# Transposes of first-stage tiles and expert blocks: 32x32 blocks on VectorE, placed by loads from DRAM

## The chip, the core and the metric

The kernel runs on one core of a Trainium2 chip. The metric is the device time of one execution in microseconds (us). The engines are TensorE (PE, its weight loads are PEld), VectorE (DVE), ScalarE (ACT), GpSimd (POOL), and SyncE (SP), which here issues most of the transfers; a queue issue stands as SPq.

## The reference

Three layers follow each other on 8 sequences of 3072 tokens with 256 channels, all in float32:

```
Y = rfft(x, axis=1) * (filt_r + 1j*filt_i);  y = irfft(Y)          # along the sequence
xn = y / sqrt(mean(y*y) + 1e-6) * rms_g                             # 24576 tokens
z  = (silu(xn @ w_gate) * (xn @ w_val)) @ w_out                     # 256 -> 1536 -> 256
e  = argmax(z @ w_route); p = softmax(z @ w_route)[e]               # 8 experts, one per token
out = p * (max(z @ w1[e], 0) @ w2[e])                               # 256 -> 1024 -> 256
```

## The kernel before

Accuracy of float32 is had by splitting each operand into a high and a low part (`split`: ACT writes the high part, DVE or POOL the difference) and by three matmuls for each product (`mm3`, lines 93 to 95).

**First stage.** The tokens go in 48 tiles of 512. For each tile the f loop has 12 turns, one for each 128 columns of the hidden layer: `gv(f)` makes 12 matmuls of 512 columns into two PSUM buffers r, `act(f)` turns them into s, ph and pl (lines 504, 505, 89, 90), and `z(f-1)` takes 12 matmuls of 264 columns with ph and pl of the turn before. PE's program therefore reads gv(f), z(f-1), gv(f+1), z(f). Beside it run the transform of the next sequence (`Job`, with forward steps, inverse steps and first steps, each with its own loads and stores on SP), and the preparation of the next tile (`Front`), in steps that a table puts on turns of the loop: `FRONT_V` holds those ahead of gv, `FRONT_P` those of PE behind z. Step 3 (turn 6) brings the tile to SBUF as x with tokens on the partitions and starts the RMS. Step 4 (turn 8) scales x by 1/rms (line 463) and has SP copy it to xc (line 468), which is the form in which PE takes it in one pass. Steps 5 and 7 (turns 9 and 10, line 478) transpose four 128x128 pieces each on PE into a PSUM buffer, and steps 6 and 8 (turns 10 and 11, lines 483 and 484) make xth on ACT and xtl on DVE from it, with rms_g. These are the moving operands of the next tile's gv. Tile 0 is prepared ahead of the loop and transposes x itself (line 480).

At the end of a tile its rows (256 values, 8 expert scores, the token's number) are scattered by POOL to zs in DRAM, sorted by expert.

**Experts.** 256 rows of one expert are a block. `run` takes the blocks in turn; each has four steps s with 12 matmuls of h and 12 of y (256 columns each), so PE's program reads h(s), y(s-1). The load of the block after next is issued in step 0 (`load`, line 731, the tile brow), behind that block's weight transfers (lines 719 and 720), which move data only where the expert changes. Step 1 transposes the next block by four 128x128 pieces on PE behind y (`tr`, line 768), step 2 splits the result into zth and ztl (`trs`), and makes the gate (`gate`, lines 753 to 761). The relu output is hh on ACT and hl on DVE (lines 785 and 786). 100 blocks run; the first four are taken from the leading expert while the last tiles are still at work.

All instructions of an engine run in the order of the program (`manual_schedule`): nothing overtakes a waiting one on the same engine. On SP this holds for the issue of transfers as well.

Of the kernel before, what the change touches and what calls it, by code (L numbers as in the profile page):

```python
# [10 lines left out]
F32 = mybir.dt.float32  # L11
# [8 lines left out]
D = 256  # L20
SEQ = 3072
FF = 1536
NE = 8
# [11 lines left out]
def fft_moe_moe_kernel(  # L35
# [33 lines left out]
    def rot():  # L69
        return psr.tile([128, 512], F32, tag="r", name="r")  # L70
# [347 lines left out]
    class Front:  # L418
# [4 lines left out]
        def step(self, k):  # L423
            if k == 0:
                z = zb[self.b]
                self.zr = []
                for a in range(2):
                    r = bp.tile([128, 2, D], F32, tag="xr", name="zr")
                    n0 = 4 * self.tau + 2 * a
                    nc.sync.dma_start(r, z[n0:n0 + 2].rearrange("n r d -> r n d"))  # L430
                    self.zr.append(r)
            elif k == 1:
                self.zh, self.zl = [], []
                for a in range(2 if self.t else 0):
                    h = bp.tile([128, 2, D], FR, tag="zh", name="zh")
                    l = bp.tile([128, 2, D], FR, tag="zl", name="zl")
                    split(h, l, self.zr[a])
                    self.zh.append(h)
                    self.zl.append(l)
            elif k == 2:  # L440
                self.q = []
                for a in range(2):
                    q = rot()
                    if self.t:
                        mm3(q, dft_h[:, 128:256], dft_l[:, 128:256], self.zh[a], self.zl[a], True, True)
                    else:
                        nc.tensor.matmul(q, lhsT=dft_raw[:, 128:256], rhs=self.zr[a], start=True, stop=True)
                    self.q.append(q)
            elif k == 3:
                self.x = bp.tile([128, 4, D], F32, tag="x", name="x", bufs=1)  # L450
                for a in range(2):
                    nc.vector.tensor_copy(self.x[:, 2 * a:2 * a + 2], self.q[a].rearrange("p (a d) -> p a d", a=2))  # L452
                ss = bp.tile([128, 4], F32, tag="ss", name="ss")
                for a in range(4):
                    junk = bp.tile([128, D], F32, tag="junk", name="junk", bufs=1)
                    nc.scalar.activation(junk, self.x[:, a], AF.Square, accum_out=ss[:, a:a + 1])
                self.ms = bp.tile([128, 4], F32, tag="ms", name="ms")
                nc.gpsimd.tensor_scalar(self.ms, ss, 1.0 / D, 1e-6, op0=ALU.mult, op1=ALU.add)
                self.ri = bp.tile([128, 4], F32, tag="ri", name="ri")
                nc.gpsimd.tensor_tensor(self.ri, self.ms, mhalf, op=ALU.pow)  # L460
            elif k == 4:
                for a in range(4):
                    nc.vector.tensor_scalar(self.x[:, a], self.x[:, a], self.ri[:, a:a + 1], None, op0=ALU.mult)
                if self.t:
                    self.xc = []
                    for a in range(2):
                        r = bp.tile([128, 2, D], F32, tag="xr", name="xc")
                        nc.sync.dma_start(r, self.x[:, 2 * a:2 * a + 2])
                        self.xc.append(r)
                self.h = bp.tile([128, 2, 512], FR, tag="xth", name="xth")  # L470
                self.l = bp.tile([128, 2, 512], FR, tag="xtl", name="xtl")
            elif k in (5, 7):
                c = (k - 5) // 2
                self.qt = rot()
                for a in range(4):
                    o, d = self.qt[:, a * 128:(a + 1) * 128], slice(c * 128, (c + 1) * 128)
                    if self.t:
                        nc.tensor.transpose(o.bitcast(FR), self.xc[a // 2][:, a % 2, d].bitcast(FR), idfr)
                    else:
                        nc.tensor.transpose(o, self.x[:, a, d], ident)  # L480
            elif k in (6, 8):
                c = (k - 6) // 2
                nc.scalar.activation(self.h[:, c], self.qt, AF.Copy, scale=rmsg[:, c:c + 1])
                nc.vector.scalar_tensor_tensor(self.l[:, c], self.qt, rmsg[:, c:c + 1], self.h[:, c].bitcast(F32), op0=ALU.mult, op1=ALU.subtract)

    class Mid:
        def __init__(self, fr):
# [212 lines left out]
    class Blk:  # L700
        def __init__(self, n):
            self.n = n
            self.side = (n + 1 - EARLY) % 2 if n >= EARLY else 0
            self.row = None

        @property
        def w(self):
# [14 lines left out]
        def load(self):  # L722
            if self.row is not None:
                return
            if self.n < EARLY:
                rb = nc.sync.value_load(esti[0:1, 0:1], min_val=0, max_val=(NE - 1) * CAP) + self.n * BLK
            else:
                i = self.n - EARLY
                rb = nc.sync.value_load(bti[i:i + 1, 0:1], min_val=0, max_val=NE * CAP)
            self.row = cpa.tile([128, 2, RW], F32, tag="row", name="brow", bufs=3)  # L730
            nc.sync.dma_start(self.row, zs[bass.ds(rb, BLK), :].rearrange("(p t) w -> p t w", t=2))

        def fresh(self):
            return self.n == 0 or self.n >= EARLY
# [12 lines left out]
            e.tensor_tensor(l, r, h.bitcast(F32), op=ALU.subtract)  # L747

        def gate(self):
            lg = self.row[:, :, D:WX]  # L750
# [10 lines left out]
            nc.vector.tensor_copy(self.id, self.row[:, :, WX])  # L761

        def tr(self):
            self.qt = rot()
            for c in range(2):
                for a in range(2):
                    j = 2 * c + a
                    nc.tensor.transpose(self.qt[:, j * 128:(j + 1) * 128].bitcast(FR), self.row[:, a, c * 128:(c + 1) * 128].bitcast(FR), idfr)

        def trs(self):  # L770
            self.zh = cpa.tile([128, 2, BLK], FR, tag="zth", name="zth")
            self.zl = cpa.tile([128, 2, BLK], FR, tag="ztl", name="ztl")
            split(self.zh, self.zl, self.qt.rearrange("p (c t) -> p c t", c=2))

        def h(self, s):
            self.q = rot()
# [32 lines left out]
                tc.add_to_no_dep_group("outs", i.ins)  # L809

    cpa = None
    blks = [Blk(n) for n in range(NBLK)]

    def early(t, f):
# [69 lines left out]
    prev.evac()  # L884

    def settle(k):
        if k == 0:
            prev.route(0)
        elif k == 1:
# [4 lines left out]
        elif k < 6:  # L894
            table(k - 2)
        elif k == 6:
            ab.close()
            cpb = ctx.enter_context(tc.tile_pool(name="cpb", bufs=1, reuse_waits="tile"))
            par[1] = wset(cpb, 1)
            sent[0] = cpb.tile([128, 2, RW], F32, name="sent")  # L900
            nc.gpsimd.memset(sent[0][:, :, 0:WX], 0.0)
            nc.gpsimd.tensor_scalar(sent[0][:, :, WX], cstt[:, 12:14], float(NTOK), None, op0=ALU.add)
# [100 lines left out]
def _constants(nb):  # L1003
# [5 lines left out]
    c[:, 4:8] = 24 * p[:, None] + np.arange(4)  # L1009
    c[:, 8] = p  # L1010
    c[:, 10] = p - 2
    c[:, 12:14] = 2 * p[:, None] + np.arange(2)
# [53 lines left out]
```

## Time and profile before

| | |
|---|---|
| median of 3 runs | 4168.78 us (4168.57 to 4171.68) |
| span of the profiled execution | 4165.9 us |
| PE busy | 4061.6 us (97%), 26476 matmuls |
| PEld busy | 3670.7 us (88%) |
| DVE busy | 2667.1 us (64%) |
| ACT busy | 2048.1 us (49%) |
| POOL busy | 1120.7 us (27%) |
| mean granted clock of TensorE | 0.989 |

The span is that of one execution on the chip, from its first to its last instruction. The busy time of an engine is the union of its instructions; a matmul's record reaches to its modelled end, so the next one starts before it is over, and the price of a matmul is better read from starts. In a timeline row the first number is the start, the second the duration (or the stretch of several merged instructions, with their count at the end), and in brackets stands how long the engine was idle before and what released it. The first stage's loop lasts to about 2975 us, the blocks from there to the end.

### The profile page before, as it was taken

The numbers are of one execution on the slowest core, as the hardware profiler recorded it, in microseconds if no ns is written. First come the engines' busy times: TensorE is split into PE (matmuls) and PEld (weight loads), VectorE is DVE, ScalarE is ACT, GpSimd is POOL, SyncE is SP. The second block draws the span as 40 slices with busy tenths as digits, with TensorE's granted clock in tenths as the row PEclk, the third lists the DMA queues.
The fourth block names the chain that finished last, engine by engine and source line by source line (L and its number), as shares of the span: only waits on it lengthen the run. The fifth ranks groups of instructions, "written<-read, shape, count | busy, mean of one in ns | idle before, by whom it ended". The sixth has DMA issues, their size and how long they took to land. (4 is left out here: it accounts for less than half of the span.)

```text
span 4165.9 us, 71195 instructions
## 1 busy us (share of the span) xinstructions
PE 4061.6 (97%) x26476; PEld 3670.7 (88%) x26476; DVE 2667.1 (64%) x5108; ACT 2048.1 (49%) x4027; POOL 1120.7 (27%) x1030
## 2 busy tenths in 40 slices
PE   4899999999999999999999999999999999999998
PEld 2688888888888888888888888888999999999998
DVE  7557657646755754774665576454477777777775
ACT  2344444444444444444444444343366666666665
POOL 5313112212212310321231122111144444444443
PEclk7899999999999999999999999999999999999999
DMA  8234233223323423322332332101222212221221
GB/s 234 90 103 116 76 91 104 82 88 86 93 80 89 106 63 96 95 79 91 100 91 68 93 99 67 47 32 37 70 68 85 87 57 77 86 87 61 70 84 39
DMA packets 196240, 350.52 MB, mean 84 GB/s; under 512 B 21930, under 2 KB 88750, under 8 KB 195888
## 3 DMA queue, kind: packets, MB, share of 16 engines
q1 hardware_dynamic: 174288, 287.33, 24.1%
q0 software_dynamic: 18816, 51.25, 3.5%
q10 hardware_dynamic: 2784, 7.34, 0.6%
q8 instruction: 210, 3.44, 0.4%
q14 instruction: 142, 1.16, 0.1%
HBM read 384.96 MB, written 105.04 MB: 118 GB/s over the span
## 5 line engine op out<-in xcount | busy, mean ns | idle before, releaser
L89 ACT ACTIVATE ph<-s 128x512 fp32r<-128x512 f32 x576 | 364.0, 632 | 1003.2 <-DVE s L505 1003.2
L505 DVE TENSOR_TENSOR s<-s,r 128x512 f32<-128x512 f32 x576 | 394.4, 685 | 524.9 <-PE r L95 497.9
L90 DVE TENSOR_TENSOR pl<-s,ph 128x512 fp32r<-128x512 f32 x576 | 439.4, 763 | 402.0 <-ACT ph L89 402.0
L95 PE MATMUL z<-wo_h,pl 128*128 128x264 f32 x2304 | 659.1, 286 | 5.2 <-DVE pl L90 5.0
L93 PE MATMUL z<-wo_h,ph 128*128 128x264 f32 x2304 | 656.3, 285 | 3.8 <-ACT ph L89 3.4
L94 PE MATMUL z<-wo_l,ph 128*128 128x264 f32 x2304 | 656.9, 285 | 0.0
L560 POOL DMA_INDIRECT zs<-row,di x192 | 206.0, 1073 | 1340.4 <-DVE di L558 635.4
L504 ACT ACTIVATE s<-r 128x512 f32<-128x512 f32 x576 | 342.6, 595 | 346.0 <-PE r L95 344.4
L93 PE MATMUL r<-xth,wg_h 128*128 128x512 f32 x1152 | 467.1, 405 | 0.4 <-DVE s L505 0.4
L93 PEld LDWEIGHTS z<-wo_h,ph 128*128 128x128 f32 x2304 | 434.7, 189 | 35.7 <-ACT ph L89 10.0
L93 PE MATMUL r<-xth,wv_h 128*128 128x512 f32 x1152 | 456.3, 396 | 2.5 <-DVE x L452 2.2
L93 PE MATMUL r<-zth,w1h 128*128 128x256 f32 x1600 | 455.6, 285 | 0.4 <-DVE hl L786 0.4
L94 PE MATMUL r<-xtl,wg_h 128*128 128x512 f32 x1152 | 455.9, 396 | 0.0
L95 PE MATMUL r<-xth,wg_l 128*128 128x512 f32 x1152 | 455.7, 396 | 0.0
L94 PE MATMUL r<-xtl,wv_h 128*128 128x512 f32 x1152 | 455.5, 395 | 0.0
L94 PEld LDWEIGHTS z<-wo_l,ph 128*128 128x128 f32 x2304 | 433.6, 188 | 24.2
L95 PE MATMUL r<-xth,wv_l 128*128 128x512 f32 x1152 | 454.6, 395 | 0.0
L94 PE MATMUL y<-w2l,hh 128*128 128x256 f32 x1600 | 450.9, 282 | 0.0
L95 PE MATMUL y<-w2h,hl 128*128 128x256 f32 x1600 | 449.9, 281 | 0.2 <-DVE hl L786 0.2
L95 PE MATMUL r<-zth,w1l 128*128 128x256 f32 x1600 | 449.5, 281 | 0.0
L93 PE MATMUL y<-w2h,hh 128*128 128x256 f32 x1600 | 448.9, 281 | 0.0
L94 PE MATMUL r<-ztl,w1h 128*128 128x256 f32 x1600 | 448.6, 280 | 0.0
(188 smaller groups left out, 9176.8 us busy)
## 6 DMA issues: line engine op xcount, KB each, us to landing
w1r<-in_w_dram SPq DMA_DIRECT2D x97, 1024.0 KB
w2r<-in_w_dram SPq DMA_DIRECT2D x97, 1024.0 KB
tab<-in_tab_dram SPq DMA_DIRECT2D x128, 528.0 KB
brow<-zs SPq DMA_DIRECT2D x100, 265.0 KB
fin<-in_x_dram SPq DMA_DIRECT2D x96, 256.0 KB
s<-fo SPq DMA_DIRECT2D x96, 256.0 KB
fin<-s SPq DMA_DIRECT2D x128, 192.0 KB
z<-fo SPq DMA_DIRECT2D x128, 192.0 KB
```

Source lines behind the costliest of these rows:

```text
L89: nc.scalar.activation(hi, src, AF.Copy)
L90: e.tensor_tensor(lo, src, hi.bitcast(F32), op=ALU.subtract)
L93: nc.tensor.matmul(o, lhsT=lh, rhs=rh, start=first, stop=False)
L94: nc.tensor.matmul(o, lhsT=lh, rhs=rl, start=False, stop=False)
L95: nc.tensor.matmul(o, lhsT=ll, rhs=rh, start=False, stop=last)
L504: nc.scalar.activation(s, self.q[0], AF.Silu)
L505: nc.vector.tensor_tensor(s, s, self.q[1], op=ALU.mult)
L560: i = nc.gpsimd.indirect_dma_start(out=zs[:, :], out_offset=bass.IndirectOffsetOnAxis(ap=di[:, t:t + 1], axis=0), in_=self.row[:, t, :], i ...
```

## The change

In a first-stage tile (but not in tile 0) step 4 now scales x and transposes it on VectorE, in 32x32 blocks, one instruction for each half of the channels, into xt. Each half goes to a buffer xs in DRAM, and four loads, one for each 32 channels of a half, bring the blocks back to where a full transpose has them, in xd. Steps 5 and 7 are gone for these tiles, and steps 6 and 8 read xd in SBUF where they read PSUM. The order of the tokens within a tile is another now, and the numbers that are written with them follow it (`_constants`).

A block from the fifth on (`turned`) is loaded in nine pieces: ext with the scores and the number, and eight of 32 partitions with 128 bytes each in zp, which place the 32x32 blocks; `tr` is then one VectorE instruction from zp to zd, and `trs` reads zd. The tiles zp and ext have three buffers in a pool of their own.

```
 (Front.step, k == 4)
-                    self.xc = []
-                    for a in range(2):
-                        r = bp.tile([128, 2, D], F32, tag="xr", name="xc")
-                        nc.sync.dma_start(r, self.x[:, 2 * a:2 * a + 2])
-                        self.xc.append(r)
+                    xs = dram.tile([128, 2, 4, 128], F32, tag="xs", name="xs", bufs=2)
+                    xd = bp.tile([128, 2, 4, 128], F32, tag="x", name="xd", bufs=1)
+                    for c in range(2):
+                        r = bp.tile([128, 4, 4, 32], F32, tag="xr", name="xt")
+                        nc.vector.transpose(r.rearrange("p j n b -> p n j b"), self.x[:, :, c * 128:(c + 1) * 128])
+                        nc.sync.dma_start(xs[:, c], r.rearrange("p j n b -> p j (n b)"))
+                    for j in range(4):
+                        nc.sync.dma_start(xd[32 * j:32 * j + 32], xs[:, :, j].rearrange("(i a) c r -> a c i r", i=4))
+                    self.xd = xd
...
-            elif k in (5, 7):
+            elif k in (5, 7) and self.t == 0:
...
+                v = self.xd[:, c].rearrange("p i r -> p (i r)") if self.t else self.qt
-                nc.scalar.activation(self.h[:, c], self.qt, AF.Copy, scale=rmsg[:, c:c + 1])
+                nc.scalar.activation(self.h[:, c], v, AF.Copy, scale=rmsg[:, c:c + 1])
...
-    FRONT_P = {5: 2, 9: 5, 10: 7}
+    FRONT_P = {5: 2}
 (Blk.load)
-            self.row = cpa.tile([128, 2, RW], F32, tag="row", name="brow", bufs=3)
-            nc.sync.dma_start(self.row, zs[bass.ds(rb, BLK), :].rearrange("(p t) w -> p t w", t=2))
+            rows = zs[bass.ds(rb, BLK), :].rearrange("(t p) w -> p t w", t=2)
...
+            self.row = turn.tile([128, 2, RW - D], F32, tag="ext", name="ext")
+            self.zp = turn.tile([128, 2, 8, 32], F32, tag="zp", name="zp")
+            nc.sync.dma_start(self.row, rows[:, :, D:RW])
+            self.ext = self.row
+            cols = zs[bass.ds(rb, BLK), :].rearrange("(q b) w -> b q w", b=32)
+            for j in range(4):
+                for c in range(2):
+                    d = c * 128 + j * 32
+                    nc.sync.dma_start(self.zp[32 * j:32 * j + 32, c], cols[:, :, d:d + 32])
 (Blk.tr)
+            if self.turned:
+                self.zd = cpa.tile([128, 2, BLK], F32, tag="zd", name="zd", bufs=1)
+                nc.vector.transpose(self.zd, self.zp)
+                return
```

On SP, the first turned tile: xs is the buffer in DRAM, xd the tile that comes back, fin the background transform's input.

```order
 L152 DMA wraw<-in_w_val_dram 128x1024 x2
-L468 DMA xc<-x 128x512 x2
+L470 DMA xs<-xt 128x512 x2
+L472 DMA xd<-xs 32x8x128 x4
 L260 DMA fin<-in_x_dram 128x512 x5
```

Two stores and four loads stand where the two copies stood, ahead of the same loads of the background.

On DVE, a later tile of the first stage, around step 4, first before, then after:

```order
L463 TENSOR_SCALAR x<-x,ri 128x256 x4
L505 TENSOR_TENSOR s<-s,r 128x512
L90 TENSOR_TENSOR pl<-s,ph 128x512
L505 TENSOR_TENSOR s<-s,r 128x512
L90 TENSOR_TENSOR pl<-s,ph 128x512
L484 SCALAR_TENSOR_TENSOR xtl<-r,rmsg,xth 128x512
```

```order
L463 TENSOR_SCALAR x<-x,ri 128x256 x4
L469 STREAM_TRANSPOSE xt<-x 128x4x4x32 x2
L507 TENSOR_TENSOR s<-s,r 128x512
L90 TENSOR_TENSOR pl<-s,ph 128x512
L507 TENSOR_TENSOR s<-s,r 128x512
L90 TENSOR_TENSOR pl<-s,ph 128x512
L486 SCALAR_TENSOR_TENSOR xtl<-xd,rmsg,xth 128x512
```

The two transposes stand between the scaling and the s of the same turn, two turns ahead of xtl.

On DVE, an expert block, steps 0 to 2, first before, then after:

```order
L803 TENSOR_SCALAR yo<-y_34994,gw 128x256
L747 TENSOR_TENSOR w1l_27585<-w1r_27588,w1h_27584 128x512 x2
L786 SCALAR_TENSOR_TENSOR hl<-r,hh 128x512
L90 TENSOR_TENSOR ztl<-r,zth 128x512
L747 TENSOR_TENSOR w2l_27587<-w2r_27589,w2h_27586 128x512
```

```order
L823 TENSOR_SCALAR yo<-y_35029,gw 128x256
L763 TENSOR_TENSOR w1l_27501<-w1r_27504,w1h_27500 128x512 x2
L806 SCALAR_TENSOR_TENSOR hl<-r,hh 128x512
L782 STREAM_TRANSPOSE zd<-zp 128x512
L90 TENSOR_TENSOR ztl<-zd,zth 128x512
L763 TENSOR_TENSOR w2l_27503<-w2r_27505,w2h_27502 128x512
```

The transpose of the next block stands between the hl of step 1 and the ztl of step 2.

## Rows read from the trace of the kernel before

**Rows 1.** Busy time by stretch: us, engines (xinstructions), granted clock, DMA share, GB/s.

```profile
400.00:2900.00 2500.00, 2485.57 (x14409) 2171.16 (x14408) 1524.42 (x2838) 1107.76 (x2179) 502.85 (x503) 1.00 0.28 82
3100.00:4000.00 900.00, 900.00 (x7665) 900.00 (x7664) 658.35 (x1380) 590.78 (x1150) 367.09 (x307) 1.00 0.25 77
```

**Rows 2.** Groups of instructions: busy us, mean ns of one, idle before.

```profile
L768 PE MATMUL r<-idfr,brow 128*128 128x128 f32 x400 | 45.8, 237 | 0.0
```

**Rows 3.** Timeline of an expert block, PE, and DVE's hl of step 2.

```profile
3407.58 0.29 PE L95 MATMUL y<-w2h,hl 128*128 128x256 f32 x1
...
3408.31 0.28 PE L95 MATMUL r<-zth,w1l 128*128 128x256 f32 x1
...
3410.37 0.69 DVE L786 SCALAR_TENSOR_TENSOR hl<-r,hh 128x512 fp32r<-128x512 f32 x1 [0.24 <-ACT hh L785]
...
3412.26 0.29 PE L95 MATMUL r<-zth,w1l 128*128 128x256 f32 x1
...
3412.63 0.28 PE L95 MATMUL y<-w2h,hl 128*128 128x256 f32 x1
```

**Rows 4.** Timeline of PE in the first stage, turns with and without transposes.

```profile
1526.33 0.29 PE L95 MATMUL z<-wo_h,pl 128*128 128x264 f32 x1
...
1527.28 0.39 PE L95 MATMUL r<-xth,wg_l 128*128 128x512 f32 x1
...
1535.58 0.28 PE L95 MATMUL z<-wo_h,pl 128*128 128x264 f32 x1
...
1536.16 0.39 PE L95 MATMUL r<-xth,wg_l 128*128 128x512 f32 x1
```

**Rows 5.** Timeline of a tile without background steps: DVE, ACT and PE.

```profile
2641.69 1.14 DVE L463 TENSOR_SCALAR x<-x,ri 128x256 f32<-128x256 f32 x4
...
2649.90 0.69 ACT L483 ACTIVATE xth<-r,rmsg 128x512 fp32r<-128x512 f32 x1 [0.35 <-PE r L478]
2651.43 0.60 ACT L504 ACTIVATE s<-r 128x512 f32<-128x512 f32 x1 [0.85 <-PE r L95]
2653.56 0.63 ACT L89 ACTIVATE ph<-s 128x512 fp32r<-128x512 f32 x1 [1.52 <-DVE s L505]
...
2657.18 0.29 PE L93 MATMUL z<-wo_h,ph 128*128 128x264 f32 x1
```

**Rows 6.** Groups of instructions on DVE: busy us, mean ns, idle before.

```profile
L347 DVE SCALAR_TENSOR_TENSOR sw<-sw,cstt,tab 96x512 f32<-96x512 f32 x112 | 124.9, 1115 | 0.0
L345 DVE STREAM_SHUFFLE sw<-r 96x512 f32<-96x512 f32 x112 | 83.0, 741 | 0.0
```

**Rows 7.** Timeline of a tile with a forward step behind the scaling: DVE and PE.

```profile
1337.39 2.94 DVE L463 TENSOR_SCALAR x<-x,ri 128x256 f32<-128x256 f32 x4
...
1344.23 0.69 DVE L90 TENSOR_TENSOR pl<-s,ph 128x512 fp32r<-128x512 f32 x1 [0.70 <-ACT ph L89]
...
1344.98 0.39 PE L95 MATMUL z<-wo_h,pl 128*128 128x264 f32 x1 [0.20 <-DVE pl L90]
```

**Rows 8.** Waits: who for whom, us in total, times, longest.

```profile
DVE gid L761 <- DMA out_dram<-yo,gid: 16.4, 16, 2.0
```

**Rows 9.** Timeline of SP and PE at the first tile: a store, its reload, first use.

```profile
139.48 0.30 SPq L375 DMA_DIRECT2D z<-fo  x1
...
141.95 0.89 SPq L430 DMA_DIRECT2D zr<-z  x2
...
145.65 3.75 PE L447 MATMUL r<-zr,dft_raw 128*128 128x512 f32 x4 [6.88 <-DMA zr<-z]
```

**Rows 10.** The page's first line, and its queues: packets, MB, share of 16 engines.

```profile
span 4165.9 us, 71195 instructions
...
q1 hardware_dynamic: 174288, 287.33, 24.1%
```

**Rows 11.** DMA of the stretch from 3.0 to 4.2 us: packets, then its one queue.

```profile
DMA packets 517, 0.06 MB, mean 49 GB/s; under 512 B 492, under 2 KB 493, under 8 KB 517
...
q1 hardware_dynamic: 517, 0.06, 47.1%
```

More of the change, by code (lines that the diff above doesn't have):

```diff
@@ L470, in step @@
+                    for j in range(4):
+                        nc.sync.dma_start(xd[32 * j:32 * j + 32], xs[:, :, j].rearrange("(i a) c r -> a c i r", i=4))
+                    self.xd = xd
                 self.h = bp.tile([128, 2, 512], FR, tag="xth", name="xth")
                 self.l = bp.tile([128, 2, 512], FR, tag="xtl", name="xtl")
-            elif k in (5, 7):
+            elif k in (5, 7) and self.t == 0:
                 c = (k - 5) // 2
                 self.qt = rot()
+                qv = self.qt.rearrange("p (i n b) -> p n i b", i=4, n=4)
@@ L475, in step @@
                 for a in range(4):
[L476 to L480, printed above, removed]
+                    nc.tensor.transpose(qv[:, a], self.x[:, a, c * 128:(c + 1) * 128], ident)
             elif k in (6, 8):
                 c = (k - 6) // 2
-                nc.scalar.activation(self.h[:, c], self.qt, AF.Copy, scale=rmsg[:, c:c + 1])
@@ L484, in step @@
-                nc.vector.scalar_tensor_tensor(self.l[:, c], self.qt, rmsg[:, c:c + 1], self.h[:, c].bitcast(F32), op0=ALU.mult, op1=ALU.subtract)
+                v = self.xd[:, c].rearrange("p i r -> p (i r)") if self.t else self.qt
+                nc.scalar.activation(self.h[:, c], v, AF.Copy, scale=rmsg[:, c:c + 1])
+                nc.vector.scalar_tensor_tensor(self.l[:, c], v, rmsg[:, c:c + 1], self.h[:, c].bitcast(F32), op0=ALU.mult, op1=ALU.subtract)
     class Mid:
@@ L704, in __init__ @@
             self.row = None
+            self.turned = n > 3
         @property
@@ L729, in load @@
                 rb = nc.sync.value_load(bti[i:i + 1, 0:1], min_val=0, max_val=NE * CAP)
-            self.row = cpa.tile([128, 2, RW], F32, tag="row", name="brow", bufs=3)
-            nc.sync.dma_start(self.row, zs[bass.ds(rb, BLK), :].rearrange("(p t) w -> p t w", t=2))
+            rows = zs[bass.ds(rb, BLK), :].rearrange("(t p) w -> p t w", t=2)
+            if not self.turned:
+                self.row = cpa.tile([128, 2, RW], F32, tag="row", name="brow", bufs=2)
+                nc.sync.dma_start(self.row, rows)
+                self.ext = self.row[:, :, D:RW]
+                return
[8 more added lines that the diff above has]
+                    nc.sync.dma_start(self.zp[32 * j:32 * j + 32, c], cols[:, :, d:d + 32])
         def fresh(self):
@@ L749, in gate @@
         def gate(self):
-            lg = self.row[:, :, D:WX]
+            lg = self.ext[:, :, 0:NE]
             m = cpa.tile([128, 2], F32, tag="gm", name="gm")
@@ L760, in gate @@
             self.id = cpa.tile([128, 2], I32, tag="gid", name="gid")
-            nc.vector.tensor_copy(self.id, self.row[:, :, WX])
+            nc.vector.tensor_copy(self.id, self.ext[:, :, NE])
         def tr(self):
+            if self.turned:
+                self.zd = cpa.tile([128, 2, BLK], F32, tag="zd", name="zd", bufs=1)
+                nc.vector.transpose(self.zd, self.zp)
+                return
             self.qt = rot()
@@ L772, in trs @@
             self.zl = cpa.tile([128, 2, BLK], FR, tag="ztl", name="ztl")
-            split(self.zh, self.zl, self.qt.rearrange("p (c t) -> p c t", c=2))
+            split(self.zh, self.zl, self.zd if self.turned else self.qt.rearrange("p (c t) -> p c t", c=2))
         def h(self, s):
@@ L811, in fft_moe_moe_kernel @@
     cpa = None
+    turn = None
     blks = [Blk(n) for n in range(NBLK)]
@@ L886, in settle @@
     def settle(k):
+        nonlocal turn
         if k == 0:
@@ L899, in settle @@
             par[1] = wset(cpb, 1)
+            turn = ctx.enter_context(tc.tile_pool(name="turn", bufs=3, reuse_waits="tile"))
             sent[0] = cpb.tile([128, 2, RW], F32, name="sent")
@@ L1008, in _constants @@
     c[:, 0] = np.where(p % 2 == 0, -1.0, 1.0)
-    c[:, 4:8] = 24 * p[:, None] + np.arange(4)
+    c[:, 4:8] = 24 * (32 * np.arange(4) + p[:, None] % 32) + p[:, None] // 32
     c[:, 8] = p
```

## The prediction

> **What bounds the kernel now.** I read the busy time by stretch first. In the 900 us of the expert stage TensorE is busy for all 900, in 2500 us of the first stage for 2485.6, so 14.4 us are idle there, and the granted clock is 1.00 in both, which is the upper of its two levels, 2.4 GHz [rows 1]. VectorE is busy 61% and 73% of the same stretches. So both stages last as long as TensorE's instruction list, as long as nothing that feeds it comes later than now. A matmul that leaves that list is worth the time by which it holds up the next ones; it is worth nothing only where another wait takes its place. Then I read what the transposes hold up, in TensorE's timeline. Last I read what stands around the places where the new work goes: VectorE and ScalarE in a first-stage tile and VectorE in an expert block.
>
> **What is removed.** From the first stage 376 transposes go, 4 at each of two places in 47 tiles: 94 groups. The blocks have 400 [rows 2], in 100 groups; the first four blocks keep theirs, so 96 groups go. The union of the busy times (45.8 us for the 400) is not the price, because matmuls overlap. I take starts instead, from the last matmul ahead of a group to the third one behind it.
> Expert block: 3407.58 to 3408.31 is 0.73 us with four transposes between; three steps without any, 3412.26 to 3412.63, take 0.37 [rows 3]. Price 0.36 us, times 96 = 34.6 us.
> First stage: 1526.33 to 1527.28 is 0.95; the same step without transposes, 1535.58 to 1536.16, is 0.58 [rows 4]. Price 0.37, times 94 = 34.8 us.
> Together 69.4 us, all of it on the path, since TensorE has no gap at these places. The two copies of x on SP go too, and one PSUM buffer per group comes free; I count neither.
>
> **What is added on VectorE.** Two block transposes of 128x512 behind the four scalings in each tile, and one in each of the 96 blocks. The trace has no such operation. Nearest is the lane shuffle of 96x512, 741 ns; above it lies the costliest 96x512 operation, 1115 ns on average; below it the scaling, four of 128x256 in 1.14 us, thus 0.57 us for 512 columns [rows 5, 6]. I take 0.74, since the shuffle is the one that moves data between lanes, with 0.57 and 1.12 as ends.
> The Trainium skill, "VectorE: DVE Perf Modes", section "The three transpose paths", gives 311 ns for a 128x128 transpose in bf16 on VectorE and, in its rules for kernel authors, advises TensorE for a 128x128 one if the result may lie in PSUM. Four times 311 ns is an estimate of 1.24 us for 512 columns; the sum with it would be 12 to 15 us less gain. No run here shows it yet.
>
> In a first-stage tile the 1.48 us push VectorE's next products back. Mostly there is idle time: in the tile at 2641 VectorE waits before its next s. In four tiles there is none (near 630, 691, 1345 and 2476 us): a forward step of the background transform stands right behind the scaling, and from 1337.39 to the end of pl at 1344.92 VectorE and the s, ph, pl chain have no slack; TensorE waits 0.20 us for this pl already [rows 7]. There all 1.48 us reach TensorE: 4 x 1.48 = 5.9 us lost (4.6 to 9.0 at the ends). Five more tiles with the same step have about 1.4 us to spare; from 0.72 us a transpose they begin to pay, up to 5 us at 1.12. That is in the range only.
>
> In an expert block the transpose stands behind one hl and ahead of ztl. The next hl ends at 3411.06 and is read first at 3412.63, 1.57 us later [rows 3]. If all 0.74 us went into that and TensorE comes 0.36 earlier, 0.47 us remain; at 1.12 still 0.09. Cost 0.
> One more place in the blocks: 16 times VectorE waits 1.0 us for a scatter before gid [rows 8], and that wait doesn't move with TensorE. There the gain may be given back: between 0 and 16 x 0.36 = 5.8 us. I take the middle, 2.9.
>
> **What is added on SP.** In a tile, six transfers stand where two stood: two stores to DRAM, which wait for VectorE, and four loads, which wait for the stores; the background's stores and loads queue behind them. In the tile at 2641 the scaling ends at 2642.83, the second transpose at 2644.3. From the issue of a store to the issue of the load that waits for it: 139.48 to 141.95, 2.47 us. From the issue of a load to the first matmul on it: 141.95 to 145.65, 3.70 us, with other loads in the queue; I take 2.47 as the lower end. Two issues take 0.89 us, so the fourth load goes out 1.35 us behind the first [rows 9]. Data there at 2644.3 + 2.47 + 1.35 + 2.47 to 3.70 = 2650.6 to 2651.8. ScalarE turns to xth at 2649.90, so it will stand 0.7 to 1.9 us. What covers that: 0.84 us up to its next s at 2651.43, and ph, which ends at 2654.19 and is read at 2657.18, 2.99 us later; TensorE comes 2 x 0.37 earlier [rows 5]. Cover 3.1 us, thus 1.2 left at worst. Cost 0; each us past the cover costs 47 us over the tiles.
> Behind these six, the background's loads slip by some 5 us; they are issued four steps ahead of use (a step is at least a 4 us turn of the f loop), and its stores have two buffers. Cost 0.
> In a block, nine transfers stand where one stood, 8 x 0.45 = 3.6 us more of SP in a block of some 11.4. The load is for the block after next, more than a block ahead of its transpose. Behind it stand the next block's weight transfers, which move data only where the expert changes. Cost 0; if that cover goes, a few us in all.
>
> **The sum.** 34.6 + 34.8 - 5.9 - 2.9 = 60.6 us. The profiled execution has a span of 4165.9 us [rows 10], the median of the runs is 4168.8, 2.9 us more, which the change doesn't touch. 4168.8 - 60.6 = 4108.2 us.
>
> **The rivals.**
> (a) Round trip too slow, the one that can end slower. If the two legs through DRAM take longer than above because stores, filter tables and spectrum traffic share the queue, data come after the cover's end. It decides at 3.1 us past 2649.90; at 4.4 us past, 1.3 x 47 = 61 us, the gain is gone; at 5.1 us past it costs 94, thus 4202 us. For it: 1.2 us is not much, and both legs are from one place. Against: the load's leg was measured beside other traffic, and where a background step lies between the scaling and xth, which it doesn't in this tile, the turns of the loop are longer.
> (b) Small pieces bound the blocks. A block's load becomes 2048 pieces of 128 bytes and 256 of 36. At the mean price of a packet of this queue, 24.1% of 16 x 4165.9 us over 174288 = 92 ns [rows 10], 2304 pieces take 13.3 us of the 16 engines. A block has 100 of the 7665 matmuls of 900 us, so it lasts 11.74 us now [rows 1] and 11.38 by the forecast: 1.9 x 96 = 182 us more, thus 4290. Against: in the 1.2 us from 3.0 on, 517 packets, 492 of them under 512 bytes, took 47.1% of the engines, 17.5 ns each [rows 11]; at that price a block takes 2.5 us.
> The Trainium skill, "DMA: Bandwidth & Descriptors", section "Specifications", names 512 bytes as the least transfer for line rate and a read-modify-write below it. By that rule the time would be (b)'s; the row on small packets speaks against it.
> (c) A dear transpose on VectorE, 1.24 us: the four tiles pay 9.9, five others 5.4, three more 2, gid 5.8: 69.4 - 23 = 46, thus 4122 us.
> (d) The change does nothing: TensorE's list gets shorter but another wait fills it. Against it are the full 900 of 900 us [rows 1]. 4169 us.
>
> **How the numbers follow.** Forecast 0.75, (c) 0.11, (a) 0.06 (half of it slower than before), (b) 0.05, (d) 0.03. Low end: transposes at 0.57 us, no loss at gid and some of the 14.4 us idle recovered, 69.4 - 4.6 + 10 = 75, thus 4094. High end: (c) with 0.3 us past the cover in all tiles, 4122 + 14 = 4136. Between them lie the forecast and (c), 0.86, of which some 0.05 may miss the ends. What a measurement of this kernel can tell from no change is about 0.2%, 8 us. Faster 0.89 (forecast, (c), and a part of (a)), same 0.03, slower 0.08.
>
> **What would show it.** The two groups of transposes gone from TensorE; the step of 0.73 us at 0.37; block transposes of 0.74 us on VectorE, 190 of them; a block of 11.38 us where it was 11.74; TensorE's wait for pl up by 6 us, in four tiles; xth waiting for xd by 0.7 to 1.9 us and no new wait on TensorE from it. Wrong if TensorE waits for ph or pl in most tiles (a), if VectorE waits for zp in the blocks (b), or if the transposes are gone and the time stays (d).

## The result, and the profile after

The changed kernel takes 4111.15 us in the median (4110.62 to 4114.23), the kernel before 4168.67 (4166.25 to 4171.68) beside it on the same chip: ratio 0.9862, 95% interval 0.9848 to 0.9876. The forecast was 4108 us. The profiled execution has a span of 4108.9 us, 57.0 less than before; the forecast was 60.6 less.

The stages first, taken from the starts of the first matmul of each tile and block in the two traces:

| stretch | before, us | after, us | gain | forecast |
|---|---|---|---|---|
| up to the first tile | 155.2 | 153.2 | 2.0 | 0 |
| first to 48th tile | 2770.4 | 2748.9 | 21.5 | 28.9 |
| 48th tile to first block | 53.9 | 53.9 | 0.0 | 0 |
| blocks 0 to 4 | 46.7 | 49.8 | -3.1 | 0 |
| blocks 4 to 99 | 1115.9 | 1079.4 | 36.5 | 31.7 |

The 2.0 us of the first row are no part of the change: in other runs with this same beginning the first tile starts anywhere from 152.3 to 155.2.

The granted clock of TensorE moves these rows too. Now and then it falls for a moment to the lower of its two levels (1.2 GHz). Counting tiles from 1, this happens in tiles 4, 33 and 38 before and in tiles 3 and 33 after (granted clock 0.97 in each of these tiles, 1.00 in the others behind the first). What it costs shows in the run with the blocks' half alone, whose first stage is that of before: there tile 38 has no such fall and is 1.51 us shorter, and tile 15 has one and is 1.53 longer. So, by this estimate, 1.5 us of the 21.5 are the clock's.

Busy time by stretch after, as in [rows 1] (us, PE, PEld, DVE, ACT, POOL, each busy with its instructions; granted clock, DMA share, GB/s):

```profile
400.00:2900.00 2500.00, 2476.58 (x14173) 2155.16 (x14172) 1570.83 (x2934) 1109.17 (x2192) 500.40 (x505) 1.00 0.32 91
3100.00:4000.00 900.00, 899.66 (x7612) 899.45 (x7611) 732.93 (x1506) 606.87 (x1189) 380.45 (x318) 1.00 0.35 80
```

TensorE is still busy for all of the expert stretch, so the blocks still last as long as its list, now without transposes. In the first stage its idle time has grown from 14.4 to 23.4 us: there something new is waited for.

The block transposes, groups of the profile (busy us, mean ns | idle before):

```profile
L782 DVE STREAM_TRANSPOSE zd<-zp 128x512 f32<-128x512 f32 x96 | 67.4, 702 | 3.7 <-DMA zp<-zs 3.6
...
L469 DVE STREAM_TRANSPOSE xt<-x 128x512 f32<-128x512 f32 x94 | 61.4, 691 | 1.6
```

Each costs 0.69 to 0.70 us. An expert block in the timeline after, to be read beside [rows 3]:

```profile
3409.93 0.28 PE L95 MATMUL y<-w2h,hl 128*128 128x256 f32 x1
...
3410.07 0.70 DVE L782 STREAM_TRANSPOSE zd<-zp 128x512 f32<-128x512 f32 x1
...
3410.30 0.28 PE L95 MATMUL r<-zth,w1l 128*128 128x256 f32 x1
...
3413.00 0.69 DVE L806 SCALAR_TENSOR_TENSOR hl<-r,hh 128x512 fp32r<-128x512 f32 x1 [0.23 <-ACT hh L805]
```

From the last y to the third matmul behind it 0.37 us pass, where 0.73 passed with four transposes between. VectorE turns the block in the meantime, and TensorE doesn't wait for it. ScalarE does, 1.4 us per block at zth (first line below), but ScalarE is not what the blocks wait for.

The waits that answer the prediction's questions (who for whom, us in total, times, longest):

```profile
ACT zth L89 <- DVE zd L782: 136.2, 96, 5.1
...
ACT xth L485 <- DMA xd<-xs: 67.1, 44, 3.9
...
PE z L93 <- ACT ph L89: 9.5, 12, 1.5
...
PE z L95 <- DVE pl L90: 5.7, 21, 1.3
...
DVE zd L782 <- DMA zp<-zs: 3.6, 1, 3.6
...
DVE gid L777 <- DMA out_dram<-yo,gid: 3.1, 2, 2.2
...
PE y L93 <- ACT hh L805: 2.4, 1, 2.4
```

Two of them in the kernel before:

```profile
PE z L95 <- DVE pl L90: 5.0, 17, 1.3
PE z L93 <- ACT ph L89: 3.4, 6, 0.9
```

ScalarE waits for the tile that comes back from DRAM in 44 of 47 tiles, 1.5 us on average. TensorE's new waits are at ph, 9.5 us where it was 3.4; at pl, where the prediction had put 6 us more, they grew from 5.0 to 5.7. VectorE waits once for zp, in block 3 for block 4, and TensorE then 2.4 us at y. The wait at gid has shrunk from 16.4 us [rows 8] to 3.1.

**Two places in the first stage.** Tiles are counted from 1 here (the expectations of the first four runs below count them from 0). In tile 20 the forward step stands behind the transposes, as in [rows 7] (timeline of DVE and PE):

```profile
1326.14 2.94 DVE L463 TENSOR_SCALAR x<-x,ri 128x256 f32<-128x256 f32 x4
...
1329.12 1.31 DVE L469 STREAM_TRANSPOSE xt<-x 128x512 f32<-128x512 f32 x2
...
1334.35 0.39 PE L93 MATMUL z<-wo_h,ph 128*128 128x264 f32 x1 [0.91 <-ACT ph L89]
...
1335.08 0.39 PE L95 MATMUL z<-wo_h,pl 128*128 128x264 f32 x1 [0.21 <-DVE pl L90]
```

TensorE waits 0.91 us for ph and 0.21 for pl, where it was 0.20 for pl alone. In tile 27 the loss has another cause (timeline of DVE, SP, ACT and PE):

```profile
1740.46 1.14 DVE L463 TENSOR_SCALAR x<-x,ri 128x256 f32<-128x256 f32 x4
...
1741.63 1.30 DVE L469 STREAM_TRANSPOSE xt<-x 128x512 f32<-128x512 f32 x2
...
1742.37 0.94 SPq L470 DMA_DIRECT2D xs<-xt  x2
...
1745.17 2.54 SPq L472 DMA_DIRECT2D xd<-xs  x4
...
1750.07 0.72 ACT L485 ACTIVATE xth<-xd,rmsg 128x512 fp32r<-128x512 f32 x1 [2.72 <-DMA xd<-xs]
...
1751.50 0.75 DVE L345 STREAM_SHUFFLE sw<-r 96x512 f32<-96x512 f32 x1
...
1756.28 0.39 PE L93 MATMUL z<-wo_h,ph 128*128 128x264 f32 x1 [0.96 <-ACT ph L89]
```

A forward step ahead of the scaling had made VectorE late. The trip through DRAM starts late with it, xth waits 2.72 us, xtl behind it, and a second forward step (from its shuffle at 1751.50) stands behind xtl. So the next ph is 0.96 us too late for TensorE.

### The profile page after: what moved, and what is told of

It reads as the page before. It is cut to its first block, busy times and chain, and to the rows that moved or that the text cites. A ratio compares the mean times of both kernels' runs of the same rounds, so it can differ in the third digit from the quotient of the medians.

```text
span 4108.9 us, 72578 instructions
## 1 busy us (share of the span) xinstructions
PE 3996.3 (97%) x25716; PEld 3600.5 (88%) x25716; DVE 2774.6 (68%) x5298; ACT 2038.4 (50%) x4027; POOL 1118.2 (27%) x1030
## 3 DMA queue, kind: packets, MB, share of 16 engines
q1 hardware_dynamic: 447120, 312.03, 29.1%
```

## The experiments

Each diff is against the changed kernel unless it says otherwise. Ratios are to the kernel before on the same chip, with the 95% interval. "Tiles" is the distance from the first to the 48th tile in the profiled execution.

### One half at a time

First stage only:

```diff
-            self.turned = n > 3
+            self.turned = False
...
-                self.row = cpa.tile([128, 2, RW], F32, tag="row", name="brow", bufs=2)
+                self.row = cpa.tile([128, 2, RW], F32, tag="row", name="brow", bufs=3)
```

> Only the first-stage part of the change; blocks are loaded whole and transposed on TensorE as before. Theory (from the two traces): the first stage gives 47 x 0.73 = 34 us less some 13 us of new waits, plus 2 us at the start, 23.5 us in all, so 4145 us; the waits in tiles 7, 8, 19 and 38 (forward step behind the scaling) and the late xd in tiles 26, 27 and 37 are there as with the whole change. The prediction's own step for this half (34.8 - 5.9 = 28.9) gives 4140. Rival: the waits in the first stage come from the blocks' part (none of it runs there), then this one shows 4135.

Measured: 4150.1 us, ratio 0.9953 (0.9937 to 0.9970), 19.5 less than before. The tiles gain 20.5, and the same eight lose as in the changed kernel.

Blocks only, with the first stage of before:

```diff
-    FRONT_P = {5: 2}
+    FRONT_P = {5: 2, 9: 5, 10: 7}
...
-                    for c in range(2):
-                        r = bp.tile([128, 4, 4, 32], F32, tag="xr", name="xt")
...
+                    for a in range(2):
+                        r = bp.tile([128, 2, D], F32, tag="xr", name="xc")
```

> Only the blocks' part; the first-stage tiles are transposed on TensorE as before. Theory: 95 blocks at 0.38 us less, less some 3 us once at the first turned block (VectorE waits 3.6 us for zp there): 33.5 us, so 4135 us; the waits for the scatter ahead of gid fall from 16 to a few as with the whole change. The prediction's own step for this half (34.6 - 2.9 = 31.7) gives 4137. Rival: the blocks gain more because tiles are earlier (an interaction of the halves), then this half alone gives under 30 us, over 4139.

Measured: 4131.9 us, ratio 0.9910 (0.9893 to 0.9927), 37.7 less. The halves add up: 19.5 + 37.7 = 57.2, against 57.5 together. So neither disturbs the other, and the shortfall lies in the first stage; block 4 loses its 3 us in the second half too.

### What the eight tiles wait for

Without the block transposes:

```diff
-                        r = bp.tile([128, 4, 4, 32], F32, tag="xr", name="xt")
-                        nc.vector.transpose(r.rearrange("p j n b -> p n j b"), self.x[:, :, c * 128:(c + 1) * 128])
-                        nc.sync.dma_start(xs[:, c], r.rearrange("p j n b -> p j (n b)"))
+                        nc.sync.dma_start(xs[:, c], self.x[:, :, c * 128:(c + 1) * 128])
```

> The whole change, but without the two VectorE transposes in a first-stage tile: x is stored to DRAM as it is and comes back by the same loads, so the tiles hold values at wrong places and the output is another. Everything else stays. Theory of two causes: the four tiles with a forward step get their 5.2 us back, and the round trip starts 1.4 us earlier, which gives back most of the 6 us in the tiles with a late xd: some 10 us, about 4101 us. If VectorE's 1.4 us are the only cause of the new waits: about 4099. If the round trip through DRAM alone is: the waits at turn 8 of tiles 7, 8, 19 and 38 stay and under 6 us come back, over 4105.

Measured: 4105.44 us, ratio 0.9844 (0.9827 to 0.9860); the tiles gain 25.6. That is 4.1 more than in the changed kernel; 1.5 of it is the fall of the clock in tile 33, which this trace doesn't have. In tiles 8, 9, 20 and 39 the wait behind the scaling goes back to what it was before, and another for late data (0.8 us in the first two, 0.2 in the others) comes up in its place. Tiles 15, 27, 28 and 38 stay late, which I had not expected: the first store is issued 0.75 us earlier, and the data come hardly earlier. Tile 27 of this kernel:

```profile
1740.90 1.14 DVE L463 TENSOR_SCALAR x<-x,ri 128x256 f32<-128x256 f32 x4
...
1742.06 1.40 SPq L468 DMA_DIRECT2D xs<-x  x2
...
1745.47 2.54 SPq L470 DMA_DIRECT2D xd<-xs  x4
...
1750.93 0.72 ACT L483 ACTIVATE xth<-xd,rmsg 128x512 fp32r<-128x512 f32 x1 [2.80 <-DMA xd<-xs]
```

From the end of the scaling to the first load it is 1745.47 - 1742.04 = 3.43 us here and 1745.17 - 1741.60 = 3.57 in the changed kernel. This store reads x in four pieces of 512 bytes per partition, not in one of 2 KB, and its leg has grown by most of what the transposes had taken. So this run takes away only one of the two causes.

Without the trip (steps 6 and 8 read the turned x where it lies):

```diff
-                        nc.sync.dma_start(xs[:, c], r.rearrange("p j n b -> p j (n b)"))
-                    for j in range(4):
-                        nc.sync.dma_start(xd[32 * j:32 * j + 32], xs[:, :, j].rearrange("(i a) c r -> a c i r", i=4))
-                    self.xd = xd
+                        self.xd.append(r)
```

> The whole change, but without the way through DRAM in a first-stage tile: VectorE transposes in 32x32 blocks and steps 6 and 8 read that result where it lies, so the blocks are at wrong places and the output is another. Two stores and four loads less per tile. Theory of two causes: some 6 us come back (tiles 14, 26, 27, 37), the waits at turn 8 of tiles 7, 8, 19 and 38 stay: about 4105 us, and ScalarE's 67 us of waiting for xd are gone. If the round trip is the only cause: about 4099. If VectorE is the only one: 4111, no change.

Measured: 4102.38 us, ratio 0.9838 (0.9821 to 0.9854); the tiles gain 29.7, 8.2 more than in the changed kernel. Both traces have two falls of the clock in their tiles. Tiles 27, 28 and 38 are on time again; tile 15 is too, but holds one of the falls. Tiles 8, 9, 20 and 39 lose what they lost. The trip costs some 8 us in tiles that the prediction didn't name, the order on VectorE some 5 in the four it did.

**Twice the transposes**, to see where VectorE's cover ends:

```diff
+                        for _ in range(2):
-                        nc.vector.transpose(r.rearrange("p j n b -> p n j b"), self.x[:, :, c * 128:(c + 1) * 128])
+                            nc.vector.transpose(r.rearrange("p j n b -> p n j b"), self.x[:, :, c * 128:(c + 1) * 128])
```

> Each block transpose of the first stage is done twice, the second over the first, so that VectorE has 1.38 us more per tile ahead of the second store. Theory of the prediction (four tiles pay in full, five with 1.4 us of slack begin to, the cover at xth is 3.1 us): the four lose 1.4 each more, 5.5; five others 1.0 to 1.4 each, 5 to 7; in the tiles without background work, where ScalarE already stands 2.0 to 3.3 us, the data come 1.4 later, past the cover by 0.3 to 1.6, 6 tiles x 0.9 = 5.5; the four late tiles 1.4 each, 5.5. Together 22 to 24: 4134 us. Rival 1, no cover at all behind the transposes: all 47 tiles pay 1.38, 65 us, 4176. Rival 2, VectorE and ScalarE have room everywhere but in the four tiles: 4117.

Measured: 4138.11 us, ratio 0.9923 (0.9907 to 0.9940). The tiles take 28.3 us more than in the changed kernel (some 3 of it are two more falls of the clock), near the 22 to 24 expected, but not where I had put all of it. About half of the tiles pay, those with background work near the step. Of the six without it only two pay, 2.25 us together where 5.5 were expected, though xth waits up to 4.7 us:

```profile
ACT xth L486 <- DMA xd<-xs: 101.0, 44, 4.7
...
PE z L93 <- ACT ph L89: 12.5, 18, 1.5
```

In five of the six xth waits 3.1 to 3.5 us and TensorE has no wait for it; in tile 43 it waits 4.7 us, and TensorE then stands 0.6. The forecast's cover of 3.1 us counts from 2649.90, where ScalarE had already stood 0.35 us [rows 5], so it allows a wait of 3.4 us, and these tiles agree with it to 0.1 us. It is not there where a forward step stands behind xtl, as in tile 27 above.

**One turn earlier:**

```diff
-    FRONT_V = {2: (0,), 4: (1,), 6: (3,), 8: (4,), 10: (6,), 11: (8,)}
+    FRONT_V = {2: (0,), 4: (1,), 6: (3,), 7: (4,), 10: (6,), 11: (8,)}
```

> Scaling, block transposes, stores and loads of x go out one turn of the f loop earlier (turn 7 instead of 8), nothing else is changed. Theory: about 6 us are lost in four tiles because x comes back from DRAM too late, and 5 us in four others because a forward step stands right behind the transposes on VectorE. One more turn of 4 us makes the data early: ScalarE's wait at xth for xd falls from 67 us in all to under 10, and the four late tiles give back 6. By the order of VectorE's instructions the forward step now stands behind the transposes in 11 tiles instead of 9, in other ones; a group of neighbours pays about 1 us in its first tile, so 4 to 9 us there instead of 5. Together 4111 - 6 + 0 to 4 = 4105 to 4109 us. Rival: the late tiles are late for ScalarE's or VectorE's own queue and not for the trip, then the waits at xd go and the time stays at 4111 or rises with the collisions to 4115.

Measured: 4123.48 us, ratio 0.9892 (0.9875 to 0.9908), 12 more than the changed kernel. The wait for the trip is gone:

```profile
ACT xth L485 <- DMA xd<-xs: 1.4, 2, 1.1
```

Tiles 9, 20 and 39 give back 1.8 us each. But seven others (5, 8, 14, 15, 16, 26 and 27), with a forward step at turn 7, now lose 1.2 to 3.0 each, 17.2 in all. Not all of this is the order: in tiles 8, 14 and 15 the granted clock is 0.95, 0.97 and 0.97 here and 1.00 in the changed kernel. By an estimate from the 1.5 us above, that is some 6 of the 17.2. The other four lose 9.5 us at 1.00. So that half of my expectation was far too low: a tile pays up to 3.0 us (tile 16), the 2.44 of scaling and transposes together and more, not only the transposes.

### The first turned block

```diff
-            self.turned = n > 3
+            self.turned = n > 4
```

> The first block turned on VectorE is number 5 instead of number 4; number 4 keeps TensorE's transposes and the single load. Theory: number 4 is the first block that is loaded after the final counts, its nine transfers end 4.7 us after they begin, and TensorE stands about 3.1 us for them; with one transfer that goes and one block's 0.36 us is given up: 4111.2 - 3.1 + 0.4 = 4108.5 us, and VectorE's wait for zp of 3.6 us is gone. Rival: the wait is the one that the stage change has in any case, or it moves to block 5: 4111 us or a little over.

Measured: 4109.4 us, ratio 0.9856 (0.9840 to 0.9873). In the trace block 3 is 3.5 us shorter and block 4 0.7, and VectorE's wait for zp is gone. The medians differ by less than their ranges; the traces settle that the wait goes. Block 4 is the first that the final counts place, so its load is issued late, and eight issues more made it too late. Part of the 4.2 us is the clock: just behind TensorE's 2.4 us at y it falls in the changed kernel (granted clock 0.94 and 0.93 in blocks 3 and 4), and here it doesn't. In the run with the step at turn 7 the same blocks are turned, TensorE stands 2.0 us there and the clock stays at 1.00: blocks 3 and 4 take 14.0 and 11.5 us, against 15.1 and 12.2 in the changed kernel and 11.6 and 11.5 here.

### What bounds a block next

Rival (b) had the small pieces as the next bound. First all eight transfers twice:

```diff
                     nc.sync.dma_start(self.zp[32 * j:32 * j + 32, c], cols[:, :, d:d + 32])
+                    nc.sync.dma_start(zq[32 * j:32 * j + 32, c], cols[:, :, d:d + 32])
```

> Each of the eight transfers of small pieces of a turned block is made twice, the second into a buffer that nobody reads: 2048 more pieces of 128 bytes per block. Theory: the pieces cost 12 to 18 ns each of one DMA engine, 2048 of them 1.5 to 2.3 us of the 16 engines in a block of 11.3 us, and eight more issues of 0.44 us on SP fit too: the share of the DMA engines in the block stage rises from 0.35 to about 0.5 and no block gets longer, but at the first turned block, whose load is late already, the issues cost 3.5 us more: 4114.7 us. Rival: pieces have a dear share that was hidden by spare engines, about 92 ns each; then blocks are bound by them and the time rises by over 50 us, to over 4160.

Measured: 4303.41 us, ratio 1.0323 (1.0306 to 1.0341), 192 more than the changed kernel. My theory of that run, that SP has room for eight more issues, is wrong, and its result looks like rival (b). The waits of SP's queue from 3100 to 4000 us say otherwise. Before the change:

```profile
SPq L720 <- DVE w2l L747: 441.3, 77, 7.0
SPq L719 <- DVE w1l L747: 94.8, 76, 1.5
SPq L720 <- POOL w2l L747: 68.5, 64, 1.1
```

and in the changed kernel:

```profile
SPq L723 <- DVE w2l L763: 127.5, 74, 2.4
SPq L723 <- POOL w2l L763: 80.8, 77, 1.1
```

In these 900 us 77 blocks are loaded before and 79 after, so SP stood (441.3 + 94.8 + 68.5) / 77 = 7.85 us per block and stands (127.5 + 80.8) / 79 = 2.64 now. With eight issues more, 0.51 us from one to the next in the timeline, it no longer stands at w2 at all. Two runs part the issues from the pieces. Eight issues of few large pieces:

```diff
                     nc.sync.dma_start(self.zp[32 * j:32 * j + 32, c], cols[:, :, d:d + 32])
+                    nc.sync.dma_start(zq[32 * j:32 * j + 32, c], rows[32 * j:32 * j + 32, c, 0:D])
```

> Each turned block gets eight more transfers, of 32 pieces of 1 KB instead of 256 pieces of 128 bytes, into a buffer that nobody reads: the same number of issues on SP as in the run of 4303 us, an eighth of its additional pieces. Theory: SP's list binds the blocks, 8 x 0.51 = 4.1 us more against 2.7 us of stand leave 1.4 us or a little more per block: 96 x 1.4 to 2.0 = 134 to 192, thus 4245 to 4303 us, and SP's waits at w2 are gone. Rival: the small pieces were the cause, then 4111 to 4120 us.

Measured: 4311.41 us, ratio 1.0345 (1.0329 to 1.0362). And one issue of 2048 small pieces:

```diff
             nc.sync.dma_start(self.row, rows[:, :, D:RW])
+            nc.sync.dma_start(zq, zs[0:2048, 0:32].rearrange("(p q) w -> p q w", q=16))
```

> Each turned block gets one more transfer, 2048 pieces of 128 bytes from a fixed place into a buffer that nobody reads: as many pieces more as in the run with all eight transfers doubled, which took 4303 us, but one issue on SP instead of eight. Theory: that run was bound by SP's list, not by the pieces: SP stands 2.7 us per block at w2 in the changed kernel (7.9 before), and 8 x 0.51 = 4.1 us more don't fit. One issue of 0.3 to 1.3 us does: the blocks keep their length, 4111 to 4115 us, with the DMA share of the block stage as high as in that run or higher. Rival: the pieces bind, then the blocks get 1.4 to 2 us longer again: 4250 to 4300 us.

Measured: 4124.33 us, ratio 0.9889 (0.9874 to 0.9905). The expert stretch of these two, first the one with large pieces, then the one with small ones:

```profile
3100.00:4000.00 900.00, 814.81 (x6389) 791.91 (x6388) 610.50 (x1270) 508.20 (x1003) 318.99 (x267) 0.96 0.39 88
```

```profile
3100.00:4000.00 900.00, 892.47 (x7517) 889.19 (x7517) 726.05 (x1489) 598.06 (x1175) 374.98 (x313) 1.00 0.50 102
```

With a DMA share of 0.50 nearly all of TensorE's matmuls fit; with 0.39, but eight issues more, 1223 of 7612 don't (the granted clock, 0.96, has fallen there too; it can explain at most 4% of them). SP's list is the next bound, not the pieces. The small pieces are not free either: the blocks lose 13.9 us and the time is 9 us above the upper end that I expected (the tiles take 3.2 us more as well, with falls of the clock in tiles 14, 15 and 38). The loss of the blocks lies at block 4 and in eight later blocks (0.6 to 2.5 us each), by the places where SP moves the weights of another expert. An issue of so many pieces keeps SP longer: from the zq issue to the end of the zp issues it is 5.7 us in the trace where the zp issues alone took 3.9, and SP's waits at w2 fall to 39 us of the 900:

```profile
SPq L723 <- POOL w2l L765: 29.8, 33, 1.1
SPq L723 <- DVE w2l L765: 9.5, 17, 0.9
```

### A table by tile

The step goes to turn 7 in the three tiles that gave 1.8 us back there, and to turn 6 in five others; block 4 stays on TensorE.

```diff
-            self.turned = n > 3
+            self.turned = n > 4
...
+    SEVEN = ({2: (0,), 4: (1,), 6: (3,), 7: (4,), 10: (6,), 11: (8,)}, {5: 2})
+    SIX = ({2: (0,), 3: (1,), 5: (3,), 6: (4,), 10: (6,), 11: (8,)}, {4: 2})
+    FRONT_T = {9: SEVEN, 20: SEVEN, 39: SEVEN, 8: SIX, 15: SIX, 27: SIX, 28: SIX, 38: SIX}
...
+        fv, fpe = FRONT_T.get(t + 1, (FRONT_V, FRONT_P))
```

> A table by tile places scaling, block transposes and transfers of x where no forward step stands right behind them on VectorE and none delays them: turn 7 instead of 8 in tiles 9, 20 and 39 (counted from 1), turn 6 in tiles 8, 15, 27, 28 and 38, with the copies of x and the transform ahead of it one turn earlier as well; all other tiles as in the changed kernel. The first block turned on VectorE is number 5. Theory: the three tiles at turn 7 give back the 1.8 us each that they gave back with all tiles at turn 7, 5.4; the five at turn 6, late by 0.9 to 2.4 us in the changed kernel, give back 4 to 8; block 4 gives back 3. From 4111: 4111 - 5.4 - 6 - 3 = 4097 us, at worst 4103 if turn 6 meets other work. Rival: the loss only moves on in each of the five, then 4103 or more.

Measured: 4092.34 us, ratio 0.9820 (0.9806 to 0.9834): 18.8 less than the changed kernel and the fastest of all. Tiles 8, 9, 15, 20, 27, 28 and 39 give back 2.65, 1.80, 1.93, 1.81, 2.06, 2.45 and 1.86 us, the blocks 4.2. The gain in tile 15 is an older wait that went, 1.6 us at the background's fl and dl; the new one at its start stays. Tile 38 gets 1.3 us longer instead. The table brings its step 1, which splits zr, from turn 4 to turn 3, and there zr has not landed: ScalarE waits 4.1 us for it, and TensorE behind ScalarE 3.5. The changed kernel has neither wait:

```profile
ACT zh L89 <- DMA zr<-z: 4.1, 1, 4.1
...
PE r L551 <- ACT s L506: 3.5, 1, 3.5
```

Right behind it the clock falls (granted clock 0.97 in tile 38, where it was 1.00; in tile 33 it is the other way round, and the 1.5 us there cancel). So in this one tile the loss only moved on, as the rival had it for all five. The waits that were new in the changed kernel are mostly gone:

```profile
PE z L95 <- DVE pl L90: 4.0, 14, 1.3
...
PE z L93 <- ACT ph L89: 2.4, 5, 0.9
```

## Why the prediction was right, and where a step failed

**TensorE's list (34.6 + 34.8).** Right in kind and size. Most tiles are 0.73 us shorter, twice 0.365: 47 x 0.73 = 34.3. A block lasts 11.35 us on average (blocks 5 to 98) where it lasted 11.75, and 11.38 was forecast.

**The term at gid (-2.9).** Not paid. The wait fell from 16.4 to 3.1 us instead of growing, and TensorE shows none of it. The blocks' half alone has 3.1 us too, in 2 waits, and the first-stage half alone 8.4 in 14. Why the scatters are now in time when the blocks end earlier, no run tells.

**The transpose on VectorE (0.74 us).** It is 0.69 to 0.70. Choosing the lane shuffle as the nearest row was right, and rival (c) falls with it. The Trainium skill, "VectorE: DVE Perf Modes", section "The three transpose paths", led to an estimate of 1.24 us from its figure in bf16; in float32 this trace measures 0.70 for 512 columns, so that estimate is refuted here.

**The four tiles (-5.9).** Named rightly, tiles 8, 9, 20 and 39, and they lose 1.59 + 0.97 + 1.33 + 1.35 = 5.2 us.

**The trip through DRAM (cost 0).** This is the step that failed. Its legs were near the estimate: in the median 2.2 us from the end of the second transpose to the first load's issue (2.47 taken), then 0.65 per further load (0.45 taken), then 3.25 from the last issue to xth (2.47 to 3.70 taken). In the six tiles without background work xth waits 2.1 to 3.2 us, above the 0.7 to 1.9 forecast (1.05 to 2.25 with the 0.35 of [rows 5]), and the cover of 3.1 us still held. But the prediction took that one tile for all, and dismissed the others with longer turns. In tiles 27, 28 and 38 a forward step ahead of the scaling makes it late, and one behind xtl makes lateness dear; tile 15 pays in its first turns for much the same in tile 14. They lose 6.4 us. With the four tiles that is 11.6 of the 12.8 that lie between 34.3 and the 21.5 measured; 0.4 are in tile 14, the rest is not assigned. Tile 38 hides more: the fall of the clock that it had before is gone, so its waits cost 2.5 us rather than 1.0, and the trip some 8, as the run without it has it. Rival (a), the trip past its cover, thus came true in these few tiles and not in most.

**Block 4.** Its 3.1 us were not foreseen; by an estimate from the run with the step at turn 7, some 0.7 of them, and 0.7 more in the row below, are the clock that fell behind the wait. The prediction weighed the nine transfers against a block's usual lead, "more than a block ahead of its transpose", and not against the first block that the counts place, whose lead is shorter.

**SP in the blocks (cost 0).** Held, but with less room than the prediction had it. 3.6 us more of SP per block were estimated; its standing time fell by 5.2. Eight issues at 0.49 to 0.51 us, each with its address arithmetic, are some 4.0 of it and the shorter block 0.4; the rest is not assigned. The 2.6 us left are five such issues. Where the expert changes there is less to spare, as the run with one issue of small pieces shows. That bound, SP's list, was not among the rivals.

**Rival (b).** Refuted, with a price for a piece. From the share of the DMA queue, after against before, (29.1% x 4108.9 - 24.1% x 4165.9) x 16 / 272832 packets is 11 ns each, the tiles' trips included. The run with the blocks' half alone moves the bytes of before in 221696 more packets: (26.3% x 4129.3 - 24.1% x 4165.9) x 16 / 221696 is 6 ns for each. Where the bytes are new too, in the run with one more issue per block, (32.9% x 4126.5 - 29.1% x 4108.9) x 16 / 198144 is 13 ns. All lie below the 17.5 ns of the lower end [rows 11]. The page's lines for it, of the changed kernel, of the blocks' half, of the run with one more issue of small pieces and of the one with eight of large ones:

```profile
q1 hardware_dynamic: 447120, 312.03, 29.1%
```

```profile
q1 hardware_dynamic: 395984, 287.38, 26.3%
```

```profile
q1 hardware_dynamic: 645264, 337.20, 32.9%
```

```profile
q1 hardware_dynamic: 483984, 337.24, 30.2%
```

The last two move the same 25.2 MB more than the changed kernel. In pieces of 128 bytes that took (32.9% x 4126.5 - 29.1% x 4108.9) x 16 = 2591 us of DMA engine, in pieces of 1 KB (30.2% x 4308.2 - 29.1% x 4108.9) x 16 = 1686: the small ones go at a rate 1.5 times lower, and that bound nothing here.

The Trainium skill, "DMA: Bandwidth & Descriptors", section "Specifications", sets 512 bytes as the least transfer for line rate. These two runs agree with it in kind.

The sum by its terms: the tiles 7.4 us below the forecast, the blocks 1.7 above (4.8 more gained, 3.1 lost at block 4), 2.0 from the beginning. 60.6 - 7.4 + 1.7 + 2.0 = 56.9 of the 57.0 measured. In the rows lies the clock as well: one fall fewer in the tiles (some 1.5 us gained), one more at block 4 (some 1.4 lost). That the total came nearer to the forecast than its parts is luck: the beginning and the blocks, 2.0 and 1.7 us the other way, made up for half of what the tiles lack.

## What to carry to other kernels

Work moved off a full engine pays by the time between its neighbours there, and that gain comes out to a few hundredths; what has to be looked for is the few places where the new work meets other work. Read the slack of a moved chain in the busiest repetition of a loop and in the first one of a stage, not in a clean one. And when one transfer becomes eight, count the issuing engine's list like any other engine's: here it had 7.9 us to spare in a block and kept 2.6.

## What the runs showed of the hardware

- A block transpose of 128x512 in float32 on VectorE takes 0.69 to 0.70 us, as much as a subtraction of that size here (0.69).
- 128-byte pieces on this queue cost 13 ns of one DMA engine each where their bytes are new, and 6 ns more packet by packet where rows that were moved anyway are cut up; 2048 of them per block (256 KB) in 8 issues fit beside everything else. The same 25.2 MB took 1.5 times as much engine time in 128-byte pieces as in pieces of 1 KB.
- One issue of 32 partitions x 8 pieces holds SP for 0.32 us and its follower comes 0.51 us later; one of 32 x 8 x 512 bytes out of DRAM holds it for 0.6 and the next comes 0.65 later.
- A store that reads four pieces of 512 bytes per partition took longer to be waited out than one that reads 2 KB: 2.85 against 2.17 us from the second store's issue to the first load's, in the median of 47 tiles (the two stores lie 0.42 us apart there and 0.60 here).
- A fall of TensorE's granted clock to the lower level in one tile cost some 1.5 us. It came right behind a wait of TensorE in tile 38 before (1.86 us) and not behind the same wait after (1.89 us), so 1.5 us between two traces can be the clock's alone.
